# Scale and offset of an activation moved from the inner block to the outputs of the second product

## The chip, the cores and the metric

The kernel runs on one core of one Trainium2 chip. The metric is the device time of one execution in microseconds; the median over several runs counts. The names of the engines in the profile: PE is TensorE's matrix product, PEld its weight load, DVE is VectorE, ACT is ScalarE, POOL is GpSimd, SP is SyncE, which here issues the transfers.

## The reference

Local attention with a few memory keys, followed by two matrix products with a squared, scaled and shifted activation between them:

```python
# q, k, v: 4 x 8 heads x 768 x 64; per chunk of 32 queries, 16 keys to the left, 8 to the right, 8 memory keys
scores = 0.125 * q_c @ k_full.T;  a = softmax(scores);  attn = a @ v_full
x = attn.transpose(0, 2, 1, 3).reshape(3072, 512)
h = x @ w_in            # 3072 x 2048
r = np.maximum(h, 0.0)
g = s * (r * r) + b     # s and b are single numbers
out = g @ w_out         # 3072 x 512
```

All in fp32. Since s and b are single numbers, `g @ w_out` equals `s * ((r * r) @ w_out) + b * colsum(w_out)`.

## The kernel before, in words

The 3072 tokens are worked on in 8 chunks of 384. For each chunk, 16 steps run over the 16 blocks `f` of 128 columns of `w_in` (128 steps `u` in all; the list `STEPS` gives their order: 8 steps of chunk 0, then the 16 of chunk 1, then the other 8 of chunk 0, then chunks 2 to 7). A step has two parts:

- `hidden(u)`: PE multiplies the chunk's x with block f of the first matrix (L510). Each fp32 number is held as a high and a low part in a reduced fp32 form, so a product is three: four times 3 products of 384 columns. The result lies in one bank of PSUM. ACT then works on it in place: relu (L517), square (L518), affine (L519, times s plus b) and copies the high part to SBUF (`high`, L520). DVE subtracts and gets the low part `gL` (`low`, L521).
- `result(u)`: PE multiplies the high and low parts of g with block f of the second matrix (L532): three tiles of 128 tokens, three products of 512 columns each, accumulated over the 16 steps of a chunk in three banks. At the chunk's last step DVE copies each bank to SBUF (`out`, L548) and SP sends it to the output. For chunk 0, whose steps are split, ACT stores the first half (L543) and DVE adds the second (L550).

The matrices come in as 64-bit numbers. For each of their 32 tiles of 128 x 1024 words, `weight` loads the words (L485), and ACT and DVE turn them into fp32 and split them into high and low parts: ACT L487 and L496, DVE L488, L490, L492, L497. The first ten use `early` buffers, the other 22 a ring of four, `words`. All tiles stay in SBUF afterwards.

The attention of a chunk is done in four pairs of heads: scores on PE (L383), maxima on DVE (L440), exponentials on ACT (L444), a small add (L447) and the normalisation (L450) on POOL, a reciprocal (L449) and transposes (L470) on DVE, values on PE (L415).

The order of instructions on each engine is laid out beforehand by `Plan.lay`, a list scheduler: each operation has an engine, an assumed duration (`HOLD`, in ns), a priority (smaller goes first; mostly the step number or a due time) and the parts that it reads and writes. Operations marked `lock` on DVE and POOL are not put at the same time in the plan:

```python
held = o.lock and e in lock and lock[other] > t
```

The chip then runs each engine's list in that order; what an instruction waits for there are its data alone. Buffers of a ring are handed out in the order in which they were asked for.

Of the kernel before, what the change touches and what calls it, by code (L numbers as in the profile page):

```python
# [11 lines left out]
F32 = mybir.dt.float32  # L12
# [3 lines left out]
AF = mybir.ActivationFunctionType  # L16
ALU = mybir.AluOpType
# [4 lines left out]
B, H, S, D = 4, 8, 768, 64  # L22
NMEM = 8
CHUNK, LEFT, RIGHT = 32, 16, 8
DM, DFF = 512, 2048
P = 128
# [5 lines left out]
NF = DFF // P  # L32
# [14 lines left out]
APART = 3.0  # L47
LEAD = 3.5
BANKS = 8
ORDER = sorted((f + half, half, f) for f in range(NF) for half in range(2))  # L50
LATE_W = [x[1:] for x in ORDER[-NEARLY:]]

# [6 lines left out]
HOLD = dict(hidden=535, result=712, scores=306, turn=84, value=254, warm=215, group=2060, group1=1230,  # L59
            relu=388, square=388, affine=570, high=388, xhigh=388, wscale=571, whigh=536, copy=270, exp=386, keep=388, store=480, bias=500,  # L60
            low=475, affine_v=475, rec=120, max=212, flip=316, xlow=470, wlow=345, wjoin=610, wsign=612, out=600,
            small=240, norm=1010, wrest=1290, issue=440)
LATE = dict(PE=230, ACT=180, DVE=180, POOL=150, SP=0)
RATE, LAND = 400.0, 2000.0
SLOW, NSLOW = 290.0, 6
# [49 lines left out]
class Plan:  # L115
# [5 lines left out]
    def op(self, eng, kind, prio, fn, reads=(), writes=(), lock=False, size=0):  # L121
        o = Op()
        o.eng, o.hold, o.fn, o.prio, o.lock, o.n, o.size = eng, HOLD[kind], fn, prio, lock, len(self.ops), size
        o.deps, o.outs, o.vals = set(), [], []
        for part in reads:
            o.deps.update(part[1])
        for part in writes:
            o.deps.update(part[1])
            o.deps.update(part[2])
        for part in reads:  # L130
            part[2].append(o)
        for part in writes:
            part[1][:] = [o]
            part[2].clear()
        o.vals = list({id(p[0]): p[0] for p in (*reads, *writes)}.values())
        for v in o.vals:
            v.left += 1
        self.ops.append(o)
        return o
# [106 lines left out]
def body(ctx: ExitStack, tc: tile.TileContext, qkv, w1, w2, out):  # L246
    nc = tc.nc
    plan = Plan()
    op = plan.op
# [4 lines left out]
    def ring(name, n, shape, dtype):  # L254
        return Ring([const.tile(shape, dtype, name=f"{name}{i}") for i in range(n)])

    def fixed():
        return Val(Ring(None))
# [5 lines left out]
    def weight_tile(half, f):  # L264
        if (half, f) not in wts:
            i = LATE_W.index((half, f)) if (half, f) in LATE_W else -1
            wts[half, f] = const.tile([P, 2, DM], F32R, name=f"w{half}_{f}", tag=f"slot{i}" if i >= 0 else f"w{half}_{f}")
        return wts[half, f]
# [13 lines left out]
    stats = Ring([tuple(const.tile([QB, GB], F32, name=f"{n}{i}") for n in ("nmax", "den", "rden")) for i in range(4)])  # L282
    gs = Ring([(const.tile([P, TOK], F32R, name=f"gH{i}"), const.tile([P, TOK], F32R, name=f"gL{i}")) for i in range(3)])
    outs = ring("partial", 3, [P, DM], F32)

    spare = [BANKS - 1]

# [18 lines left out]
        nc.tensor.matmul(idle, ones[:, :P], ones, start=True, stop=True)  # L306


    c_id, c_aT, c_mask, c_s, c_b = (fixed() for _ in range(5))
    op("ACT", "copy", -100, lambda: nc.scalar.activation(s_sb, ones[:, :1], AF.Exp), (), (c_s[0],))  # L310
    op("POOL", "copy", -100, lambda: make_identity(nc, ident), (), (c_id[0],))
    def constants():
# [164 lines left out]
    def weight(i, half, f, due):  # L477
        src = (w1, w2)[half][f]
        raw = Early(i, 0, 2 * DM) if i < NEARLY - 6 else Val(words)
        v, w = Val(wvs), c_w[half, f]  # L480
        both = lambda: raw.tile.bitcast(I32).rearrange("p (n two) -> p n two", two=2)
        lo, hi = (lambda: both()[:, :, 0]), (lambda: both()[:, :, 1])
        bits = lambda: v.tile.bitcast(I32)
        dst = lambda a: weight_tile(half, f)[:, a, :]
        op("SP", "issue", due - 4, lambda: nc.sync.dma_start(both(), src), (), (raw["lo"], raw["hi"]), size=P * DM * 8)  # L485

        op("ACT", "wscale", due, lambda: nc.scalar.activation(v.tile, hi().bitcast(F32), AF.Copy, scale=2.0 ** -112), (raw["hi"],), (v[0],))  # L487
        op("DVE", "wlow", due, lambda: nc.vector.tensor_scalar(lo(), lo(), 29, None, ALU.logical_shift_right),  # L488
           (), (raw["lo"],), lock=True)
        op("DVE", "wjoin", due, lambda: nc.vector.scalar_tensor_tensor(bits(), bits(), 3, lo(), ALU.logical_shift_left, ALU.bitwise_or),  # L490
           (raw["lo"],), (v[0],), lock=True)
        op("DVE", "wsign", due, lambda: nc.vector.scalar_tensor_tensor(bits(), hi(), -2147483648, bits(), ALU.bitwise_and, ALU.bitwise_or),  # L492
           (raw["hi"],), (v[0],), lock=True)
        rest = half or f >= N0
        old = list(c_early[LATE_W.index((half, f))].parts.values()) if (half, f) in LATE_W else []
        op("ACT", "whigh", due, lambda: nc.scalar.activation(dst(0), v.tile, AF.Copy), (v[0],), [w["H"], *old])  # L496
        op("DVE", "wjoin", due, lambda: nc.vector.tensor_tensor(  # L497
            dst(1), v.tile, dst(0).bitcast(F32), ALU.subtract), (v[0], w["H"]), (w["L"],), lock=True)


    g_vals, h_vals, a_vals, partial = {}, {}, {}, {}

    def hidden(u):
        ch, f = STEPS[u]
        h = Val(ps, "h")
        x, w = x_vals[ch], c_w[0, f]

        def products(c):
            for n, (wi, xi) in enumerate(((0, NC_T + c), (1, c), (0, c))):
                nc.tensor.matmul(h.tile[:, :TOK], weight_tile(0, f)[:, wi, c * P:(c + 1) * P], x.tile[xi], start=(c == 0 and n == 0),  # L510
                                 stop=(c == NC_T - 1 and n == 2))

        for c in range(NC_T):
            op("PE", "hidden", u, lambda c=c: products(c), (x["H", c], x["L", c], w["H"], w["L"]), (h[0],))
        g = g_vals[u] = Val(gs)
        hp = lambda: h.tile[:, :TOK]
        op("ACT", "relu", u, lambda: nc.scalar.activation(hp(), hp(), AF.Relu), (), (h[0],))  # L517
        op("ACT", "square", u, lambda: nc.scalar.activation(hp(), hp(), AF.Square), (), (h[0],))  # L518
        op("ACT", "affine", u, lambda: nc.scalar.activation(hp(), hp(), AF.Identity, scale=s_sb, bias=b_sb), (c_s[0], c_b[0]), (h[0],))  # L519
        op("ACT", "high", u, lambda: nc.scalar.activation(g.tile[0], hp(), AF.Copy), (h[0],), (g["H"],))  # L520
        op("DVE", "low", u, lambda: nc.vector.tensor_tensor(g.tile[1], hp(), g.tile[0].bitcast(F32), ALU.subtract),  # L521
           (h[0], g["H"]), (g["L"],))

    def result(u):
        ch, f = STEPS[u]
        g, w = g_vals[u], c_w[1, f]
        first = u == 0 or STEPS[u - 1][0] != ch
        last = u + 1 == len(STEPS) or STEPS[u + 1][0] != ch

        def products(acc, t):  # L530
            for n, (gi, wi) in enumerate(((1, 0), (0, 1), (0, 0))):
                nc.tensor.matmul(acc.tile, g.tile[gi][:, t * P:(t + 1) * P], weight_tile(1, f)[:, wi, :], start=(first and n == 0), stop=(last and n == 2))  # L532

        for t in range(NT):
            if first:
                a_vals[t] = Val(ps, "acc")
            acc = a_vals[t]
            op("PE", "result", u + LAG - 0.1, lambda acc=acc, t=t: products(acc, t), (g["H"], g["L"], w["H"], w["L"]), (acc[0],))
            if not last:
                continue  # L540
            if f < NF - 1:
                o = partial[t] = Val(outs)
                op("ACT", "store", u, lambda acc=acc, o=o: nc.scalar.activation(o.tile, acc.tile, AF.Copy), (acc[0],), (o[0],))  # L543
                continue
            o = partial[t] if not ch else Val(wvs if ch == 1 else outs)
            ot = lambda o=o: o.tile
            if ch:
                op("DVE", "out", u, lambda acc=acc, ot=ot: nc.vector.tensor_copy(ot(), acc.tile), (acc[0],), (o[0],))  # L548
            else:
                op("DVE", "out", u, lambda acc=acc, ot=ot: nc.vector.tensor_tensor(ot(), acc.tile, ot(), ALU.add), (acc[0],), (o[0],))  # L550
            row = ch * TOK + t * P
            op("SP", "issue", u, lambda ot=ot, row=row: nc.sync.dma_start(out[row:row + P, :], ot()), (o[0],), (), size=P * DM * 4)

# [3 lines left out]
    made, pairs = {0}, set()  # L557
    for i, (due, half, f) in enumerate(ORDER):
        weight(i, half, f, due - 1.5)
    for u, (ch, f) in enumerate(STEPS):  # L560
        if ch not in made:
            made.add(ch)
            for c in range(H // 2):
                if (ch, c) not in pairs:
                    attend(ch, c)
            if open_ and ch + 1 < NCHUNK:
                pairs.add((ch + 1, 0))
                attend(ch + 1, 0)
            elif open_:
                open_.pop()[4]()  # L570
        hidden(u)
        result(u)
# [41 lines left out]
```

## Time and profile before

| | us |
|---|---|
| median of 3 runs | 642.14 (641.97 to 642.25) |
| span of the profiled execution | 639.8 |
| PE busy | 625.7 |
| ACT busy | 422.4 |
| DVE busy | 354.8 |
| POOL busy | 86.9 |

The page gives the span of the profiled execution, from its first to its last instruction, and no other time for it; the median of the runs lies 2.3 us above the span. In the page's second part each digit is the busy share, in tenths, of one of 40 equal slices of the span. In rows of groups the columns are line, engine, operation, output and input, shapes, count, then total busy time, mean ns of one, and the idle time before them with what ended it. In rows of the timeline and of the chain of waits the first number is the start in us, the second the duration.

### The profile page before, as it was taken

The numbers are of one execution on the slowest core, as the hardware profiler recorded it, in microseconds if no ns is written. First come the engines' busy times: TensorE is split into PE (matmuls) and PEld (weight loads), VectorE is DVE, ScalarE is ACT, GpSimd is POOL, SyncE is SP. The second block draws the span as 40 slices with busy tenths as digits, with TensorE's granted clock in tenths as the row PEclk, the third lists the DMA queues.
The fourth block names the chain that finished last, engine by engine and source line by source line (L and its number), as shares of the span: only waits on it lengthen the run. The fifth ranks groups of instructions, "written<-read, shape, count | busy, mean of one in ns | idle before, by whom it ended". The sixth has DMA issues, their size and how long they took to land.

```text
span 639.8 us, 10842 instructions
## 1 busy us (share of the span) xinstructions
PE 625.7 (98%) x3822; PEld 544.2 (85%) x3826; DVE 354.8 (55%) x1283; ACT 422.4 (66%) x1137; POOL 86.9 (14%) x140
## 2 busy tenths in 40 slices
PE   9998988999999999999999999999999999999997
PEld 5686877888888898888888988889888888989995
DVE  5999999726667355563447554473555725421112
ACT  6999898756766566666566666664666665645543
POOL 4522100101211011110011111110111100100000
PEclk9999999999999999999999999999999999999999
DMA  8933664012112011121103011120111200010001
GB/s 336 404 112 114 212 207 152 2 46 83 58 46 96 5 41 47 47 95 47 45 2 105 37 46 46 46 96 1 45 47 47 96 17 1 1 50 1 1 0 50
DMA packets 17334, 46.83 MB, mean 73 GB/s; under 512 B 1920, under 2 KB 1920, under 8 KB 17280
## 3 DMA queue, kind: packets, MB, share of 16 engines
q1 hardware_dynamic: 17280, 46.15, 20.8%
q8 instruction: 30, 0.49, 0.3%
q14 instruction: 24, 0.20, 0.1%
HBM read 39.85 MB, written 6.29 MB: 72 GB/s over the span
## 4 chain that ended last, share of the span: by engine, by line
PE 80%; DVE 10%; ACT 6%; DMA 4%; issue 1%; SPq 0%; POOL 0%; DVEq 0%
PE ps L532 37%; PE ps L510 36%; PE ps L383 4%; PE ps L415 3%; DVE wv L490 2%; DVE w L497 2%; DVE wv L492 2%; DMA early<-w 2%; ACT t L444 1%; DMA v<-qkv 1%; DVE gL L521 1%; DVE words L488 1%; ACT wv L487 1%; DMA early<-qkv 1%; ACT ps L519 1%; ACT w L496 1%
## 5 line engine op out<-in xcount | busy, mean ns | idle before, releaser
L510 PE MATMUL ps<-xH,w 128*128 128x384 f32 x1024 | 261.8, 337 | 1.3 <-DVE w L497 1.3
L532 PE MATMUL ps<-w,gH 128*128 128x512 f32 x768 | 240.0, 393 | 0.6 <-DVE w L497 0.5
L510 PEld LDWEIGHTS ps<-xH,w 128*128 128x128 f32 x1024 | 186.0, 188 | 7.6 <-DVE w L497 2.4
L521 DVE TENSOR_TENSOR gL<-ps,gH 128x384 fp32r<-128x384 f32 x128 | 70.6, 552 | 208.8 <-ACT gH L520 207.6
L517 ACT ACTIVATE ps<-ps 128x384 f32<-128x384 f32 x128 | 60.9, 475 | 173.1 <-PE ps L510 173.1
L510 PE MATMUL ps<-xL,w 128*128 128x384 f32 x512 | 174.4, 341 | 0.0
L532 PEld LDWEIGHTS ps<-w,gH 128*128 128x128 f32 x768 | 144.0, 188 | 29.4 <-DVE w L497 1.3
L532 PE MATMUL ps<-w,gL 128*128 128x512 f32 x384 | 154.9, 403 | 6.6 <-DVE gL L521 6.6
L470 DVE STREAM_TRANSPOSE aT<-t 32x128 f32<-32x128 f32 x384 | 116.2, 303 | 51.1 <-POOL t L450 46.4
L444 ACT ACTIVATE t<-t,nmax 96x128 f32<-96x128 f32 x256 | 99.3, 390 | 17.2 <-DVE nmax L440 16.9
L510 PEld LDWEIGHTS ps<-xL,w 128*128 128x128 f32 x512 | 96.1, 188 | 6.6 <-ACT w L496 0.4
L532 PEld LDWEIGHTS ps<-w,gL 128*128 128x128 f32 x384 | 72.0, 188 | 24.5 <-DVE gL L521 9.6
L519 ACT ACTIVATE ps<-ps,b_sb,s_sb 128x384 f32<-128x384 f32 x128 | 82.6, 645 | 4.2
L450 POOL TENSOR_TENSOR t<-t,rden 96x512 f32<-96x512 f32 x64 | 68.5, 1070 | 85.8 <-DVE rden L449 85.8
L447 POOL TENSOR_SCALAR rden<-den 96x4 f32<-96x4 f32 x64 | 16.0, 251 | 375.5 <-ACT t L444 372.8
L520 ACT ACTIVATE gH<-ps 128x384 fp32r<-128x384 f32 x128 | 62.9, 491 | 3.9
L518 ACT ACTIVATE ps<-ps 128x384 f32<-128x384 f32 x128 | 60.8, 475 | 4.0
L440 DVE CUSTOM_DVE_ANT_0 t<-ps,mask 96x128 f32<-96x128 f32 x256 | 56.8, 281 | 4.2 <-PE ps L383 3.8
L444 ACT ACTIVATION_READ_ACCUMULATOR t<-t,nmax 96x1 f32 x256 | 48.1, 188 | 0.0
L383 PE MATMUL ps<-raw 64*96 64x128 f32 x448 | 31.8, 279 | 0.0
L383 PEld LDWEIGHTS ps<-raw 64*96 64x96 f32 x448 | 25.3, 159 | 4.1 <-issue 0.8
L415 PEld LDWEIGHTS ps<-aT,v 128*64 128x64 f32 x448 | 19.6, 136 | 7.9 <-issue 6.6
(45 smaller groups left out, 289.3 us busy)
## 6 DMA issues: line engine op xcount, KB each, us to landing
raw<-qkv SPq DMA_DIRECT2D x28, 448.0 KB, 3.3
words<-w SPq DMA_DIRECT2D x22, 512.0 KB, 3.9
v<-qkv SPq DMA_DIRECT2D x28, 256.0 KB, 3.6
out<-partial SPq DMA_DIRECT2D x21, 256.0 KB, 2.1
early<-w SPq DMA_DIRECT2D x10, 512.0 KB, 9.9
early<-qkv SPq DMA_DIRECT2D x3, 448.0 KB, 5.8
early<-qkv SPq DMA_DIRECT2D x4, 256.0 KB, 6.4
out<-wv SPq DMA_DIRECT2D x3, 256.0 KB, 3.8
```

Of the source, the lines that this page charges most:

```text
L383: nc.tensor.matmul(scv(n)[:, j, :], raw.tile[rows, j * QB:(j + 1) * QB], raw.tile[rows, TOK + j * P:TOK + (j + 1) * P], start=True, stop=True)
L440: op("DVE", "max", a + 0.1, lambda j=j: nc.vector.tensor_tensor_reduce(t.tile[:, j, :], scv()[:, j, :], mask[:, kind(j)], -SCALE, 3.0e38, ...
L444: op("ACT", "exp", a + 0.2, lambda j=j: nc.scalar.activation(t.tile[:, j, :], t.tile[:, j, :], AF.Exp, bias=nmax()[:, j:j + 1], scale=-1.0 ...
L450: op("POOL", "norm", a + 0.25, lambda: nc.gpsimd.tensor_tensor(t.tile, t.tile, rden().unsqueeze(2).to_broadcast([QB, GB, P]), ALU.mult), [ ...
L470: nc.vector.transpose(aT.tile[gg, :, cs], t.tile[cs, :, gg])
L510: nc.tensor.matmul(h.tile[:, :TOK], weight_tile(0, f)[:, wi, c * P:(c + 1) * P], x.tile[xi], start=(c == 0 and n == 0), stop=(c == NC_T - ...
L517: op("ACT", "relu", u, lambda: nc.scalar.activation(hp(), hp(), AF.Relu), (), (h[0],))
L518: op("ACT", "square", u, lambda: nc.scalar.activation(hp(), hp(), AF.Square), (), (h[0],))
L519: op("ACT", "affine", u, lambda: nc.scalar.activation(hp(), hp(), AF.Identity, scale=s_sb, bias=b_sb), (c_s[0], c_b[0]), (h[0],))
L520: op("ACT", "high", u, lambda: nc.scalar.activation(g.tile[0], hp(), AF.Copy), (h[0],), (g["H"],))
L521: op("DVE", "low", u, lambda: nc.vector.tensor_tensor(g.tile[1], hp(), g.tile[0].bitcast(F32), ALU.subtract), (h[0], g["H"]), (g["L"],))
L532: nc.tensor.matmul(acc.tile, g.tile[gi][:, t * P:(t + 1) * P], weight_tile(1, f)[:, wi, :], start=(first and n == 0), stop=(last and n == 2))
```

## The change

`affine` on ACT goes. Its factor s is applied where the accumulators are read, at the outputs (DVE) and at chunk 0's stores (ACT). Its offset b becomes a row that is added to every output, `bc`: b times the column sums of the second matrix. POOL adds up the 16 converted tiles of the second matrix (15 adds of 128 x 1024, into a buffer of the `words` ring), two fp32 products with a matrix of ones sum over the 128 rows on PE, and ACT multiplies by b. These carry the priority 24. For chunk 0 the offset is added on POOL before the transfer.

```diff
+DUE_SUM = 24.0
...
-            small=240, norm=1010, wrest=1290, issue=440)
+            small=240, sum=2150, columns=1706, norm=1010, wrest=1290, issue=440)
...
+    bc = const.tile([P, DM], F32, name="bc")
+    ones_f = nc.const_aps.tensor(1.0, [P, P], F32)
...
+    def sums():
+
+        total, all_ = Val(words), Val(ps, "v")
+        flat = lambda f: weight_tile(1, f).bitcast(F32).rearrange("p a n -> p (a n)")
+        part = lambda f: (c_w[1, f]["H"], c_w[1, f]["L"])
+        op("POOL", "sum", DUE_SUM, lambda: nc.gpsimd.tensor_tensor(total.tile, flat(0), flat(1), ALU.add), part(0) + part(1), (total[0],), lock=True)
+        for f in range(2, NF):
+            op("POOL", "sum", DUE_SUM, lambda f=f: nc.gpsimd.tensor_tensor(total.tile, total.tile, flat(f), ALU.add), part(f), (total[0],), lock=True)
+
+        def products():
+            for a in range(2):
+                nc.tensor.matmul(all_.tile, ones_f, total.tile[:, a * DM:(a + 1) * DM], start=a == 0, stop=a == 1)
+
+        op("PE", "columns", DUE_SUM, products, (total[0],), (all_[0],))
+        op("ACT", "store", DUE_SUM, lambda: nc.scalar.activation(bc, all_.tile, AF.Identity, scale=b_sb), (all_[0], c_b[0]), (c_bc[0],))
...
-        op("ACT", "affine", u, lambda: nc.scalar.activation(hp(), hp(), AF.Identity, scale=s_sb, bias=b_sb), (c_s[0], c_b[0]), (h[0],))
...
-                op("ACT", "store", u, lambda acc=acc, o=o: nc.scalar.activation(o.tile, acc.tile, AF.Copy), (acc[0],), (o[0],))
+                op("ACT", "store", u, lambda acc=acc, o=o: nc.scalar.activation(o.tile, acc.tile, AF.Identity, scale=s_sb),
+                   (acc[0], c_s[0]), (o[0],))
...
-                op("DVE", "out", u, lambda acc=acc, ot=ot: nc.vector.tensor_copy(ot(), acc.tile), (acc[0],), (o[0],))
+                op("DVE", "out", u, lambda acc=acc, ot=ot: nc.vector.scalar_tensor_tensor(ot(), acc.tile, s_sb, bc, ALU.mult, ALU.add),
+                   (acc[0], c_s[0], c_bc[0]), (o[0],))
...
-                op("DVE", "out", u, lambda acc=acc, ot=ot: nc.vector.tensor_tensor(ot(), acc.tile, ot(), ALU.add), (acc[0],), (o[0],))
+                op("DVE", "out", u, lambda acc=acc, ot=ot: nc.vector.scalar_tensor_tensor(ot(), acc.tile, s_sb, ot(), ALU.mult, ALU.add),
+                   (acc[0], c_s[0]), (o[0],))
+                op("POOL", "norm", u + 1, lambda ot=ot: nc.gpsimd.tensor_tensor(ot(), ot(), bc, ALU.add), (c_bc[0],), (o[0],), lock=True)
...
     for i, (due, half, f) in enumerate(ORDER):
         weight(i, half, f, due - 1.5)
+    sums()
```

More of the change, by code (lines that the diff above doesn't have):

```diff
@@ L306, in warm @@
         nc.tensor.matmul(idle, ones[:, :P], ones, start=True, stop=True)
-    c_id, c_aT, c_mask, c_s, c_b = (fixed() for _ in range(5))
+    c_id, c_aT, c_mask, c_s, c_b, c_bc = (fixed() for _ in range(6))
     op("ACT", "copy", -100, lambda: nc.scalar.activation(s_sb, ones[:, :1], AF.Exp), (), (c_s[0],))
```

## The prediction

> **What bounds the kernel now.** I read the page's first two parts, then the chain of waits, piece by piece for the first 120 us.
>
> ```profile
> span 639.8 us, 10842 instructions
> PE 625.7 (98%) x3822; PEld 544.2 (85%) x3826; DVE 354.8 (55%) x1283; ACT 422.4 (66%) x1137; POOL 86.9 (14%) x140
> ...
> PE   9998988999999999999999999999999999999997
> ...
> DVE  5999999726667355563447554473555725421112
> ACT  6999898756766566666566666664666665645543
> ...
> PEclk9999999999999999999999999999999999999999
> ...
> PE 80%; DVE 10%; ACT 6%; DMA 4%; issue 1%; SPq 0%; POOL 0%; DVEq 0%
> ```
>
> The span is 639.8 us; the median of the runs is 642.14 us, so 2.3 us lie around it, and I add every change to 642.14. TensorE (PE) looks full throughout, with an undisturbed clock, but the chain gives it 80%, not 98%: in the first seven slices (16 us each) ScalarE (ACT) and VectorE (DVE) are full too. The pieces of the chain show who hands over to whom:
>
> ```profile
> 31.32 0.64 ACT ps L519
> ...
> 35.63 0.65 ACT ps L519
> ...
> 41.28 0.65 ACT ps L519
> ...
> 49.77 0.55 ACT ps L519
> ...
> 53.86 0.65 ACT ps L519
> ...
> 55.09 0.69 DVE w L497
> ...
> 112.45 0.48 DVE gL L521
> ...
> 112.97 2.33 PE ps L532 x9
> ...
> 117.41 2.09 PE ps L532 x9
> ...
> 140.21 2.29 PE ps L532 x9
> ```
>
> So there are three stages: ACT sets the pace to 55 us, DVE (the conversion of the weights) to 113 us, and PE from there to the end. L519 is the affine step that goes. It is worth something only where ACT is on this chain, and in the tail.
>
> **The affine step, removed.** Over the whole kernel it is 82.6 us of ACT:
>
> ```profile
> L519 ACT ACTIVATE ps<-ps,b_sb,s_sb 128x384 f32<-128x384 f32 x128 | 82.6, 645 | 4.2
> DVE w L497 <- ACT w L496: 1.7, 3, 1.2
> DVE gL L521 <- ACT gH L520: 0.9, 2, 0.7
> ```
>
> The last two rows are DVE's waits in the window 8 to 115 us. In the PE stage the step is hidden by PE, and its removal gives nothing. In the first 55 us five of them, 0.64 + 0.65 + 0.65 + 0.55 + 0.65 = 3.1 us, lie on the chain. But DVE is next: its work up to 113 us stays as it is, so a faster ACT can shorten this stretch only by the time that DVE waits for ACT, 1.7 + 0.9 = 2.6 us. Ends 0 (the planner spends it on another order) and 2.6; I take 2.3, since 3.1 us removed exceeds the sum of the waits, and leave 0.3 for gaps of the new order.
>
> In the tail the last hidden block goes through relu, square, affine, high and low before PE may go on:
>
> ```profile
> 631.97 0.65 ACT L519 ACTIVATE ps<-ps,b_sb,s_sb 128x384 f32<-128x384 f32 x1
> 632.39 0.63 PE L532 MATMUL ps<-w,gH 128*128 128x512 f32 x2
> 633.78 0.50 PE L532 MATMUL ps<-w,gL 128*128 128x512 f32 x1 [0.76 <-DVE gL L521]
> ```
>
> PE waits 0.76 us there, longer than the 0.65 removed: gain 0.65.
>
> **The two fp32 products with the ones, added on PE.** They fall in the stage where PE is full, so their whole time counts. No 128x128 fp32 product of 512 columns is in the trace; the nearest row is the fp32 score product:
>
> ```profile
> 139.10 1.12 PE L383 MATMUL ps<-raw 64*96 64x128 f32 x16
> ```
>
> Sixteen of 64 rows, issued in pairs for the two halves of the array: eight pairs, 0.14 us per 128 columns. Two products of 512 columns over all rows are then 8 x 0.14 = 1.1 us. That is the lower end. Upper end: the entry columns=1706 in the diff, plus the 0.2 us by which the nine result products take longer behind an fp32 group (2.29 against 2.09): 1.9. I take 1.7, as this product is twice as high and fills the array alone. The Trainium skill, "FP8 and Floating Point Precision", section TensorE Precision Notes, says that true fp32 makes four passes; with the 2.09 us for nine results an estimate is 2 x 4 x 0.23 = 1.9 us. By that the sum would be 0.2 us higher; no row here shows a full-height fp32 product.
>
> **The sums on GpSimd, added.** Fifteen adds of 128x1024. Their duration comes from the normalisation and the small add:
>
> ```profile
> L450 POOL TENSOR_TENSOR t<-t,rden 96x512 f32<-96x512 f32 x64 | 68.5, 1070 | 85.8 <-DVE rden L449 85.8
> L447 POOL TENSOR_SCALAR rden<-den 96x4 f32<-96x4 f32 x64 | 16.0, 251 | 375.5 <-ACT t L444 372.8
> 105.83 0.69 DVE L492 SCALAR_TENSOR_TENSOR wv<-words,wv 128x512 int32<-128x512 int32 x1
> 117.69 0.22 POOL L447 TENSOR_SCALAR rden<-den 96x4 f32<-96x4 f32 x1 [49.60 <-ACT t L444]
> 156.15 0.68 DVE L548 COPY wv<-ps 128x512 f32<-128x512 f32 x1
> ```
>
> Twice 1070 ns is 2.1 us; by the slope between the two rows, (1070 - 251) / 508 = 1.6 ns an element, 0.25 + 1.65 = 1.9. Fifteen are 28 to 32 us. The total needs a words buffer, and it is the last in line: it gets the one of the nineteenth of 22 loads, whose last reader is the L492 at 105.83. So the adds can start at about 106.5, on a GpSimd (POOL) that sits idle for 49.6 us until 117.69. With the two pairs of small add and normalisation that come in between (2 x 2 x 1.3 us) they end at about 140 to 145; products and store make it 148. The first reader of bc is the output of step 23, at 156.15: some 8 us to spare. Behind that output on DVE wait the next maxima and gL, and for its bank of PSUM the next accumulation. I cost this wait at nothing, under the cover of these 8 us.
>
> What the adds do to DVE while weights are still being converted is the open cost. The planner keeps certain POOL and DVE instructions apart (lock), but only in its own plan; on the chip the adds are held by data alone. What an overlap costs:
>
> ```profile
> 36.73 1.04 POOL L450 TENSOR_TENSOR t<-t,rden 96x512 f32<-96x512 f32 x1 [1.15 <-DVE rden L449]
> 37.35 0.97 DVE L497 TENSOR_TENSOR w<-wv,w 128x512 fp32r<-128x512 f32 x1
> 39.45 0.69 DVE L490 SCALAR_TENSOR_TENSOR wv<-wv,early 128x512 int32<-128x512 int32 x1
> 39.52 1.52 POOL L450 TENSOR_TENSOR t<-t,rden 96x512 f32<-96x512 f32 x1 [0.29 <-DVE rden L449]
> 161.00 2.52 DVE L470 STREAM_TRANSPOSE aT<-t 32x128 f32<-32x128 f32 x8 [1.16 <-POOL t L450]
> 161.06 0.22 POOL L447 TENSOR_SCALAR rden<-den 96x4 f32<-96x4 f32 x1
> ```
>
> Where POOL was first, L497 took 0.97 instead of 0.69 us and ended 0.55 us behind POOL's end at 37.77; where DVE was first, POOL took 1.52 instead of 1.04. So the two wait for each other whole. The transposes do not take part (0.22 beside them, as alone), so the adds after the weights cost DVE nothing. Between 106.5 and 116 us DVE has a dozen instructions that do. But the late weights serve steps 20 and up and have time; what PE needs is gL, which does not wait for POOL unless it stands behind one that does:
>
> ```profile
> 107.04 0.55 DVE L521 TENSOR_TENSOR gL<-ps,gH 128x384 fp32r<-128x384 f32 x1
> ...
> 115.22 0.55 DVE L521 TENSOR_TENSOR gL<-ps,gH 128x384 fp32r<-128x384 f32 x1
> ```
>
> Its product runs at 117.41, so this last gL has 1.6 us of slack. The first add (2.1 us) falls at the gL of 107.04, and DVE has maxima ready that do not contend. Ends: 0 (one add there, filled) and 3 x 2.1 - 1.6 = 4.7 (three more adds ahead of the small add at 117.69). Nearest is the pair of rows above, where DVE lost 0.3 of POOL's 1.04 us; 0.3 of three adds is 1.9, less part of the slack: I take 1.0.
>
> **The small edits.**
>
> ```profile
> L550 DVE TENSOR_TENSOR partial<-ps,partial 128x512 f32<-128x512 f32 x3 | 1.9, 685 | 0.0
> L548 DVE COPY partial<-ps 128x512 f32<-128x512 f32 x18 | 11.7, 686 | 3.3 <-PE ps L532 3.2
> ```
>
> Outputs: DVE now reads a second tensor and a scalar, and 685 against 686 says that this costs nothing, in the tail too. The three stores of chunk 0 with a scale may cost ACT something, but they fall in the stage in which DVE sets the pace: nothing. The add of bc to chunk 0 on POOL (three of about 1.1 us) delays only output transfers in SP's queue, whose next loads are far ahead of need: nothing. One PSUM bank for the column sums for some 2 us can move an attention group by a step: nothing, PE has other work.
>
> **The sum.** -2.3 - 0.65 + 1.7 + 1.0 = -0.25: 641.9 us.
>
> **Rivals.** (1) Faster: DVE's waits go whole and the adds find DVE busy with what does not contend: -2.6 - 0.65 + 1.4 + 0 = -1.9, 640.3. For it: the maxima that wait for a free DVE and the weights' spare time. Best corner, with 1.1 on PE: 640.0. (2) Slower, by the lock: if the plan puts two or more further adds ahead of POOL's first small add, the chip runs them back to back from 106.5, and DVE's weight instructions, with gL behind them, stand still: -1.25 + 4.7 gives 645.6 with three, -1.25 + 2.6 gives 643.5 with two; with one or none it is covered. The rule behind it is in the Trainium skill, "SBUF — State Buffer", section Who interferes with whom: whichever issues first keeps the shared port pair for its whole instruction and the other fully blocks. The rows at 37 and 39 us agree. (3) Slower, by the new wait: if the adds take 2.5 us (15 x 0.5 = 7.5 us more) and DVE holds POOL up by 3.5 us more, bc is 3 us late, the output of step 23 waits for it and PE for the output's bank: 644.9. (4) It does not do what it says: the planner's new order loses the 2.3 us at the start, and DVE paces as before: 644.2.
>
> **Numbers.** About 0.2%, 1.3 us, is what a measurement here can tell from no change. Forecast (640.9 to 643.4) 0.36; rival 1 0.32; rival 2 0.20; rival 3 0.05; rival 4 0.07. Faster 0.32, same 0.36, slower 0.32. The forecast's own range is 640.9 to 643.4. For 8 in 10 the range goes from just below the best corner, 639.6, to just past rival 2 with three adds, 646.0.
>
> **What would show it.** The chain passes from ACT to DVE earlier than 55 us and from DVE to PE near 111 us; DVE's waits for ACT before that are near zero; PE waits less than 0.2 us at the end; two products of some 1.7 us together stand near 146 us with PE full around them. Weight instructions of DVE of 1.5 to 2.8 us beside long adds would show rival 2; a DVE output waiting for ACT's bc, rival 3. I am wrong if the adds start much earlier or later than 106 us, or take other than about 2 us, or if the new order leaves PE gaps after 120 us.

## The result, and the profile after

The changed kernel takes 714.51 us (median; 714.34 to 714.96) against 642.19 us: ratio 1.113, 95% interval 1.112 to 1.115. It is 72 us slower; forecast were 641.9 us and a range that ended at 646.0. The direction was that of some of the rivals, the size that of none.

The page of the changed kernel, first two parts and the chain:

```profile
span 712.2 us, 10776 instructions
PE 630.7 (89%) x3829; PEld 547.5 (77%) x3833; DVE 381.9 (54%) x1283; ACT 346.2 (49%) x1010; POOL 128.5 (18%) x158
...
PE   9987100279999999999999999999999999999997
...
DVE  5999999353116767344735473556555564422112
ACT  6977630083335645554444453455445554433332
POOL 4510049730001213011101120111111111100000
PEclk9999655599999999999999999999999999999999
...
PE 79%; DVE 9%; POOL 6%; ACT 3%; DMA 2%; issue 1%; SPq 0%; DVEq 0%; POOLq 0%; ACTq 0%
```

ACT is relieved as intended (346.2 us busy instead of 422.4), and PE has 5 us more to do. But in slices 5 to 8 (18 us each) PE does next to nothing, and POOL, with 6% on the chain, is new there. The waits name it, and PE's and POOL's timelines show it (start, duration, instruction; in brackets the idle time before):

```profile
PE ps L515 <- POOL words L511: 64.5, 1, 64.5
```

```profile
72.98 0.63 PE L551 MATMUL ps<-w,gH 128*128 128x512 f32 x2
138.08 3.78 PE L515 MATMUL ps<-words,const-float32-1.0 128*128 128x512 f32 x4 [64.48 <-POOL words L511]
141.66 1.49 PE L462 MATMUL ps<-ident,t 96*128 96x96 f32 x8
```

```profile
98.37 2.40 POOL L509 TENSOR_TENSOR words<-w,w 128x1024 f32<-128x1024 f32 x1 [58.52 <-ACT wv L490]
100.84 37.19 POOL L511 TENSOR_TENSOR words<-words,w 128x1024 f32<-128x1024 f32 x14
```

One wait of 64.5 us: after the eight steps of chunk 0 PE stands at the column products until POOL has added all 16 tiles. The third row of PE says why nothing else is done meanwhile: chunk 1's transposes (L462) come right behind the column products. In the kernel before, all eight groups of them (L459) ran between 27 and 69 us; here none runs between 26 and 141 us.

The cause is in `sums()` and in the way in which `Ring` hands out buffers. Banks of PSUM of one kind are given in the order in which they were asked for (`self.next.get(v.kind, 0) == v.n`). The column sums ask for a bank of kind "v" with `Val(ps, "v")`, and `sums()` is called ahead of the loop in which chunk 1 asks. The transposes and values of the attention use kind "v" too. So in the plan no transpose of chunk 1 can have a bank before the column products have had theirs, and these wait for the last weight and 15 adds. The chip then keeps the plan's order. The second half of chunk 0 cannot fill the gap either: its hidden blocks ask for banks of kind "h" behind those of chunk 1.

DVE's rows at that place show the second effect, which the prediction had as a rival:

```profile
97.55 0.69 DVE L495 SCALAR_TENSOR_TENSOR wv<-words,wv 128x512 int32<-128x512 int32 x1
98.15 0.42 DVE L491 TENSOR_SCALAR words<-words 128x512 int32<-128x512 int32 x1
98.60 2.71 DVE L493 SCALAR_TENSOR_TENSOR wv<-wv,words 128x512 int32<-128x512 int32 x1
101.24 2.82 DVE L500 TENSOR_TENSOR w<-wv,w 128x512 fp32r<-128x512 f32 x1
103.98 2.83 DVE L495 SCALAR_TENSOR_TENSOR wv<-words,wv 128x512 int32<-128x512 int32 x1
106.74 2.56 DVE L491 TENSOR_SCALAR words<-words 128x512 int32<-128x512 int32 x1
```

From the first add on, the same DVE instructions take 2.6 to 2.8 instead of 0.4 to 0.7 us: each waits for most of an add, and the adds, with 37.19 / 14 = 2.66 us instead of 2.40, wait for DVE in turn. So on the chip an instruction waits not for its data alone, as the section on the kernel before has it: DVE and POOL also wait for each other. The Trainium skill, "SBUF — State Buffer", section Who interferes with whom, has this as a lock that the first holds for its whole instruction while the other fully blocks; 2.82 - 0.69 = 2.1 us, most of an add, agrees.

### The profile page after: what moved, and what is told of

It is laid out like the page before. It is cut to its first block, busy times and chain, and to the rows that moved or that the text cites. A ratio compares the mean times of both kernels' runs of the same rounds, so it can differ in the third digit from the quotient of the medians.

```text
span 712.2 us, 10776 instructions
## 1 busy us (share of the span) xinstructions
PE 630.7 (89%) x3829; PEld 547.5 (77%) x3833; DVE 381.9 (54%) x1283; ACT 346.2 (49%) x1010; POOL 128.5 (18%) x158
## 4 chain that ended last, share of the span: by engine, by line
PE 79%; DVE 9%; POOL 6%; ACT 3%; DMA 2%; issue 1%; SPq 0%; DVEq 0%; POOLq 0%; ACTq 0%
PE ps L551 36%; PE ps L530 35%; POOL words L511 5%; PE ps L386 4%; PE ps L418 3%; DVE wv L493 3%; DVE w L500 2%; DVE wv L495 2%; DMA early<-w 1%; ACT t L447 1%; DVE words L491 1%; DMA early<-qkv 1%; DVE gL L540 1%; PE ps L515 1%; DVE t L443 1%
## 5 line engine op out<-in xcount | busy, mean ns | idle before, releaser
L515 PE MATMUL ps<-words,const-float32-1.0 128*128 128x512 f32 x4 | 3.8, 1100 | 64.5 <-POOL words L511 64.5
L511 POOL TENSOR_TENSOR words<-words,w 128x1024 f32<-128x1024 f32 x14 | 36.2, 2583 | 1.1
L499 ACT ACTIVATE w<-wv 128x512 fp32r<-128x512 f32 x32 | 20.1, 629 | 25.2 <-DVE wv L495 24.7
```

Source lines behind the costliest of these rows:

```text
L511: op("POOL", "sum", DUE_SUM, lambda f=f: nc.gpsimd.tensor_tensor(total.tile, total.tile, flat(f), ALU.add), part(f), (total[0],), lock=True)
```

## The experiments

**The line of banks.** `own_bank` gives the column sums a kind of their own, which also takes them out of the limit on how many banks the attention may hold:

```diff
+        if kind == "c":
+            return True
         return n("h", 0) < 2
...
-        total, all_ = Val(words), Val(ps, "v")
+        total, all_ = Val(words), Val(ps, "c")
```

> The changed kernel, but the bank of PSUM for the column sums is asked for in a line of its own instead of the line in which the transposes and values of the attention ask. Theory A (the line: the column sums were asked for ahead of chunk 1's attention, banks of a line are handed out in the order asked, so chunk 1's transposes and values cannot be planned before the column sums): PE no longer stops for 64 us, the time comes back to 642 to 648 us. Rival B (the 15 adds and the DVE instructions that wait for them hold PE up by themselves): the adds still take some 40 us and the time stays above 690 us.

Measured: 648.95 us (ratio to the kernel before 1.011, 1.010 to 1.013). That is as theory A said: 65.6 of the 72 us go with the line. A loss of 7 us stays. `asked_later`, below, keeps the kind and the limit and moves the place alone.

`no_adds` keeps the line, and leaves out 14 of the 15 adds:

```diff
-            ... flat(0), flat(1), ALU.add), part(0) + part(1), (total[0],), lock=True)
-        for f in range(2, NF):
-            op("POOL", "sum", ...)
+            ... flat(NF - 1), flat(NF - 2), ALU.add), part(NF - 1) + part(NF - 2), (total[0],), lock=True)
```

> The changed kernel with the line of banks as it is, but 14 of the 15 adds left out: the total is the sum of the last two tiles alone (the column sums are wrong by the rest). Theory A: PE still stops before the column sums, now until the last weight tiles are converted and one add is done, near 110 us instead of 138: about 685 us. Rival B: without the adds PE is not held up, 640 to 646 us.

Measured: 687.94 us (one run), near the 685 of theory A. PE's timeline in this kernel:

```profile
108.14 3.78 PE L513 MATMUL ps<-words,const-float32-1.0 128*128 128x512 f32 x4 [35.31 <-POOL words L509]
111.72 1.49 PE L462 MATMUL ps<-ident,t 96*128 96x96 f32 x8
```

PE still stops, for 35.3 us, and the transposes still stand behind. So of the wait of 64.5 us some 35 are for the last weights and one add, and 29 for the adds that follow and slow the last weights down.

`asked_later` is the changed kernel with `sums()` called once chunk 1's attention has asked for its banks:

```diff
-    sums()
     for u, (ch, f) in enumerate(STEPS):
...
+        if u == starts[1]:
+            sums()
         hidden(u)
```

> The changed kernel with the column sums asked for at another place: after chunk 1's attention instead of before it, in the same line of banks as it was. Theory A (the place in the line decides who has to wait): chunk 1 is free, now the attention of chunk 2 stands behind the column sums; it is needed later, so the loss is a fraction of the 65 us: 650 to 660 us. Rival B (what counts is only that the column sums use a bank of that line at all): above 690 us.

Measured: 659.95 us (one run), at the edge of what A said. No wait for the column products is left, but the time is 11 us more than in `own_bank`: now chunk 2's attention is late, and PE waits for gL behind it three times between 167 and 198 us:

```profile
169.18 0.50 PE L551 MATMUL ps<-w,gL 128*128 128x512 f32 x1 [2.03 <-DVE gL L540]
183.48 0.80 PE L551 MATMUL ps<-w,gL 128*128 128x512 f32 x1 [2.04 <-DVE gL L540]
197.80 0.50 PE L551 MATMUL ps<-w,gL 128*128 128x512 f32 x1 [2.13 <-DVE gL L540]
```

With the same kind and the same limit, the place in the line alone is worth 714.51 - 659.95 = 54.6 us.

**The affine step.** `no_affine` is the kernel before without it:

```diff
-        op("ACT", "affine", u, lambda: nc.scalar.activation(hp(), hp(), AF.Identity, scale=s_sb, bias=b_sb), (c_s[0], c_b[0]), (h[0],))
```

> The kernel before with the affine step left out and nothing in its place (s and b are missing from the result). What its removal alone is worth. The prediction's terms say -2.3 us at the start and -0.65 us in the tail: 639.2 us. Rival: the planner's new order does not use the time at the start, only the tail gains: 641.5 us.

Measured: 639.82 us (ratio 0.997, 0.996 to 0.998): -2.0 us where the terms said -2.95. DVE's waits for ACT in the window 8 to 115 us, and PE at 83 us and, in the last two rows, in the tail:

```profile
DVE gL L520 <- ACT gH L519: 0.5, 2, 0.3
...
DVE w L497 <- ACT w L496: 0.4, 1, 0.4
```

```profile
83.01 0.50 PE L531 MATMUL ps<-w,gL 128*128 128x512 f32 x1 [2.14 <-DVE gL L520]
83.34 0.83 PE L531 MATMUL ps<-w,gH 128*128 128x512 f32 x2
83.97 0.63 PE L531 MATMUL ps<-w,gL 128*128 128x512 f32 x1
84.40 1.05 PE L531 MATMUL ps<-w,gH 128*128 128x512 f32 x2
...
631.25 0.63 PE L531 MATMUL ps<-w,gH 128*128 128x512 f32 x2
631.96 0.50 PE L531 MATMUL ps<-w,gL 128*128 128x512 f32 x1
```

DVE's waits for ACT fell from 2.6 to 0.9 us, and PE's gap in the tail from 0.76 to 0.08 us. The two are worth 2.4 us. Against that stands a gap of 2.1 us at 81 us that the kernel before did not have, where the new order puts a gL late, and behind it products that take 0.63 instead of 0.40 us: the granted clock is 0.57 in the 4 us after it. What this gap costs in the end is not shown. PE's waits for gL over the whole kernel fell all the same, as these rows of the kernel before and of `no_affine` show (us in total, times, longest):

```profile
PE ps L532 <- DVE gL L521: 6.6, 9, 0.9
PE ps L531 <- DVE gL L520: 4.3, 5, 2.1
```

**What the products and the small edits cost.** `own_no_adds` is `own_bank` without 14 of the adds, the one that is left being of the last two tiles.

> late_adds with 14 of the 15 adds left out (the column sums hold the last two tiles only); the two products, the store and the new outputs stay. Against no_affine (639.8 us) it shows what the products and the other small edits cost: theory A 1.9 us for the two products, 641 to 642 us. If it is as late_adds, the adds after the weights cost nothing; if it is at 640 or below, the products are hidden after all.

Measured: 642.04 us (ratio 1.000, 0.999 to 1.001): 2.2 us over `no_affine`. The products of `own_bank`, at full clock, are 1.88 us:

```profile
157.63 1.88 PE L517 MATMUL ps<-words,const-float32-1.0 128*128 128x512 f32 x4
```

They are not hidden. The 0.3 us that is left for the other edits is no more than the runs of one kernel differ by. With the bank and the adds out of the way the change is worth nothing: -2.0 + 2.2.

**The adds.** So the adds cost `own_bank` 648.95 - 642.04 = 6.9 us. Its rows on DVE, POOL and PE:

```profile
109.65 0.68 DVE L502 TENSOR_TENSOR w<-wv,w 128x512 fp32r<-128x512 f32 x1
110.25 2.63 DVE L493 TENSOR_SCALAR words<-words 128x512 int32<-128x512 int32 x1
...
114.25 2.62 DVE L493 TENSOR_SCALAR words<-words 128x512 int32<-128x512 int32 x1
```

```profile
109.67 2.92 POOL L513 TENSOR_TENSOR words<-words,w 128x1024 f32<-128x1024 f32 x1
112.68 1.01 POOL L452 TENSOR_SCALAR rden<-den 96x4 f32<-96x4 f32 x2
113.76 2.82 POOL L513 TENSOR_TENSOR words<-words,w 128x1024 f32<-128x1024 f32 x1
```

```profile
121.60 0.80 PE L553 MATMUL ps<-w,gL 128*128 128x512 f32 x1 [5.42 <-DVE gL L542]
122.19 1.05 PE L553 MATMUL ps<-w,gH 128*128 128x512 f32 x2
```

```profile
121.00:126.00 5.00, 4.40 (x11) 3.54 (x12) 3.84 (x13) 0.63 (x1) 3.84 (x3) 0.50 0.00 0
```

Two DVE instructions wait 2.2 us each for an add, gL stands behind them, and PE is idle for 5.4 us (4.4 of them for these two waits, the other 1.0, by this difference, for the plan's order); then its clock is 0.50 for the next 5 us (the last row is the window of all engines, the clock is its third number from the end).

`late_adds` moves the adds so that they meet no such DVE instruction:

```diff
-            ... flat(0), flat(1), ALU.add), part(0) + part(1), ...
-        for f in range(2, NF):
+            ... flat(NF - 1), flat(NF - 2), ALU.add), part(NF - 1) + part(NF - 2), ...
+        for f in range(NF - 2):
```

> own_bank with the adds in another order: the first add takes the last two tiles of the second matrix, so no add can start before the weights are converted, and no add meets a DVE instruction that shares the port. Theory A (own_bank's excess of some 7 us over the kernel before is DVE held up by the adds at 107 to 117 us, PE idle behind it for 5.4 us and at half clock for 5 us more): the gap goes, 641 to 643 us. Rival B (the excess is the new order of the plan, or the output of step 23 waiting for bc, which now comes later): 645 us or more.

Measured: 649.4 us (ratio 1.012, 1.010 to 1.013). Not as A said, though the gap that A named is gone. Two others came:

```profile
150.28 0.50 PE L553 MATMUL ps<-w,gL 128*128 128x512 f32 x1 [1.45 <-DVE gL L542]
...
158.79 3.45 PE L517 MATMUL ps<-words,const-float32-1.0 128*128 128x512 f32 x4 [4.04 <-POOL words L513]
```

```profile
129.20 19.75 POOL L513 TENSOR_TENSOR words<-words,w 128x1024 f32<-128x1024 f32 x8
149.04 0.51 POOL L452 TENSOR_SCALAR rden<-den 96x4 f32<-96x4 f32 x2
```

```profile
149.29 0.47 DVE L454 RECIPROCAL rden<-rden 96x4 f32<-96x4 f32 x2 [7.10 <-POOL rden L452]
149.68 0.54 DVE L542 TENSOR_TENSOR gL<-ps,gH 128x384 fp32r<-128x384 f32 x1
```

An add takes 19.75 / 8 = 2.47 us, so 15 of them, with the attention's POOL work among them, last from 116.8 to 158.7 us, and PE reaches its column products 4 us too early; behind this wait they take 3.45 instead of 1.88 us. The first gap comes from the adds too: POOL's small add (L452) stands behind eight of them, DVE's reciprocal waits 7.1 us for it, and gL stands behind the reciprocal. The gaps and the longer products make 1.45 + 4.04 + 1.57 = 7.1 us, of 649.4 - 642.04 = 7.4 over `own_no_adds`. So B's half sentence on lateness was right, with the column products and not the output of step 23 as the place. Started early, the adds meet DVE; started late, they do not finish in time.

`half_adds` tests the second: the same order with adds of half the width (only the high parts) and one product. The planner's durations for them are halved too (1250 and 853 ns).

```diff
-        flat = lambda f: weight_tile(1, f).bitcast(F32).rearrange("p a n -> p (a n)")
+        flat = lambda f: weight_tile(1, f)[:, 0, :].bitcast(F32)
...
+        half = lambda: total.tile[:, :DM]
...
-            for a in range(2):
-                nc.tensor.matmul(all_.tile, ones_f, total.tile[:, a * DM:(a + 1) * DM], start=a == 0, stop=a == 1)
+            nc.tensor.matmul(all_.tile, ones_f, half(), start=True, stop=True)
```

> late_adds with adds of half the width: only the high parts of the tiles are summed, the low parts are left out of the column sums, and one product takes the place of two. The adds still start after the weights are converted. Theory A (late_adds pays 6.9 us over own_no_adds because 15 full adds of 2.45 us cannot be done between the last weight at 117 us and the place of the column sums near 155 us; with 1.2 to 1.3 us each they are done near 140): PE's gap of 4 us goes; own_no_adds (642.0) less one product (0.9) is 641.1 us. Rival B (adds beside the attention cost by their number, or delay its normalisation, whatever their length): 643 us or more.

Measured: 641.0 us (ratio 0.998, 0.997 to 0.999), as A said (its 6.9 us for `late_adds` is `own_bank`'s number; it should be 7.4). PE's gaps at 116, 149 and 155 us are gone, and the adds are short:

```profile
126.07 13.62 POOL L514 TENSOR_TENSOR words<-words,w 128x512 f32<-128x512 f32 x10
```

So the loss of `late_adds` is the length of its adds. That the loss of `own_bank` is its early adds rests on the rows above and on the gap at 116 us, which is gone when they start later.

**PE's clock in the long wait.** `warm_wait` is the changed kernel with idle products in front of the column sums:

```diff
         def products():
+            for _ in range(280):
+                nc.tensor.matmul(all_.tile, ones[:, :P], ones, start=True, stop=True)
             for a in range(2):
```

> The changed kernel with 280 idle products (bf16 ones, into the bank that the column sums use next) in PE's queue ahead of the column sums, about 61 of the 64 us that PE waits there. Nothing else is moved. Theory A: part of the 72 us is PE's clock, at 0.50 after the wait; with PE busy the column products take 1.9 instead of 3.8 us and the attention behind them runs at full clock: 710 to 712 us. Rival B: behind the wait PE is held by other engines, so a faster clock shortens nothing but the column products, or not even these: 713 to 714.5 us.

Measured: 714.99 us, with runs from 712.92 to 716.52, so unclear. The idle products ended 3.2 us too soon, and the clock was down again (0.63 from 138 to 142 us). A share of the clock in the 72 us is not shown. In the changed kernel the clock is 0.50 from 138 to 142 us and 0.87 in the next 4 us, so an estimate of the most that it can be is 4 x 0.50 + 4 x 0.13 = 2.5 us. Why the runs of `warm_wait` differ by more than those of the others was not tried; over the whole run the granted clock was 0.998 in the two shorter ones and 0.990 in the two longer.

**A version without column sums.** `fold_b` is the kernel before without the affine step; b/s is added where the high and low parts are made, and s multiplies the outputs (one DVE reciprocal and one product of 128 x 1 at the start give b/s):

```diff
-        op("ACT", "affine", ...)
-        op("ACT", "high", u, lambda: nc.scalar.activation(g.tile[0], hp(), AF.Copy), (h[0],), (g["H"],))
-        op("DVE", "low", u, lambda: nc.vector.tensor_tensor(g.tile[1], hp(), g.tile[0].bitcast(F32), ALU.subtract), ...)
+        op("ACT", "ghigh", u, lambda: nc.scalar.activation(g.tile[0], hp(), AF.Identity, bias=b_sb), (h[0], c_b[0]), (g["H"],))
+        op("DVE", "low", u, lambda: nc.vector.scalar_tensor_tensor(g.tile[1], hp(), b_sb, g.tile[0].bitcast(F32), ALU.add, ALU.subtract), ...)
...
-                op("DVE", "out", u, lambda acc=acc, ot=ot: nc.vector.tensor_copy(ot(), acc.tile), ...)
+                op("DVE", "out", u, lambda acc=acc, ot=ot: nc.vector.tensor_scalar(ot(), acc.tile, s_sb, None, ALU.mult), ...)
```

> The kernel before without the affine step; instead b/s is added where the high part is copied (a bias on ACT) and where the low part is formed (a scalar in the DVE instruction), and s multiplies the outputs. No column sums, no adds, no extra product. If the affine step is worth what the prediction said and the bias costs ACT little: 639.5 us. If the bias makes the high copy longer by as much as a quarter of the affine step or the planner's order is worse: 641 to 642 us.

Measured: 639.38 us (ratio 0.996, 0.995 to 0.997), faster than the kernel before and the changed one. Groups of this kernel:

```profile
L523 DVE SCALAR_TENSOR_TENSOR gL<-ps,b_sb,gH 128x384 fp32r<-128x384 f32 x128 | 78.3, 612 | 200.2 <-ACT gH L522 174.4 <-PE ps L534 25.0
...
L522 ACT ACTIVATE gH<-ps,b_sb 128x384 fp32r<-128x384 f32 x128 | 74.4, 581 | 4.1
```

The two that take the scalar in are 0.06 to 0.09 us longer (552 and 491 ns before), and the affine step's 645 ns is gone. Its 639.38 us are no more than the 639.82 of `no_affine`, which leaves s and b out.

## Why the prediction was wrong

- **The bank (the step that failed).** The prediction put a term at nothing: "One PSUM bank for the column sums for some 2 us can move an attention group by a step: nothing." I costed the bank by how long it is held. What it cost was its place: 65.6 us (`own_bank`). For the buffer of `words` I had used the same rule, that the total is the last in line; for the banks I did not ask who stands behind. It was to be read from the code alone, and no row of the profile before shows it.
- **The affine step.** -2.3 and -0.65 were said, -2.0 in all was measured (`no_affine`). The waits of DVE for ACT went as described, though not whole (1.7 of 2.6 us), and the tail gained its 0.7. The 0.4 us between these 2.4 and the 2.0 may be the new order's gap at 81 us and the clock behind it, for which the prediction had left 0.3 us; that is not shown.
- **The products.** 1.7 said, 1.88 in the trace, and 2.2 in the time together with the small edits. The four passes of the Trainium skill, "FP8 and Floating Point Precision", section TensorE Precision Notes, gave 1.9, nearer than the row that I took as the lower end.
- **The adds and the lock.** 1.0 said, 6.9 measured. The mechanism was rival 2's, with 2.2 us for each DVE instruction that meets an add; in `own_bank` two did, and PE was idle for 5.4 us. But rival 2 asked for two further adds ahead of POOL's first small add and called one covered; in `own_bank` one stands there (109.67, the small add at 112.68) and one behind. The 0.3 of an add was misread: L497 at 37.35 came 0.42 us before POOL's end, so its row shows the rest of one instruction and not a share; the two in `own_bank` came 0.5 to 0.6 us into an add. Too small was the cover: gL had 1.6 us of slack in the kernel before, and none in the new order. The clock behind an idle PE, some 2 us (0.50 for 5 us with PE 4.4 us busy), was not in the sum at all.
- **The adds' length.** 1.9 to 2.1 us were said, 2.47 measured. An end at 140 to 145 us became 156 (`own_bank`) and 159 (`late_adds`); in `own_bank` 5.6 us of that is POOL waiting for DVE's reciprocal before 122 us. So the cover of 8 us under which the new wait cost nothing was not there. In `own_bank` PE still did not wait, for the plan had its column products at 157.63; `late_adds`, whose adds start 10 us later, shows that wait. That "the adds after the weights cost DVE nothing" did not hold there either: the transposes kept their pace (2.52 us for eight at 129 us), but the reciprocal waited for POOL's small add behind the adds, and gL with it.
- **The outputs.** 685 against 686 ns said that a second tensor costs nothing; with the scalar it is 746 (L570 of `own_bank`). In `fold_b` an output with the scalar and no second tensor takes 746 as well, so it goes with the scalar.

From the changed kernel over `own_bank`, `own_no_adds` and `no_affine` to the kernel before, the steps are bank 65.6, adds 6.9, products and the rest 2.2, affine step -2.0. Being differences between neighbours they must add up to the whole (72.7 us; 72.3 with the kernel before as it was measured beside the changed one), so their sum proves nothing by itself.

## What to carry to other kernels

Where a planner hands out buffers in the order in which they were asked for, a new user's cost is not how long it holds one but who asked after it and what it waits for itself: find that line before costing anything else. Before moving work off a busy engine, see whether it can be folded into instructions that exist on both sides (here a bias and a scalar operand) instead of into new ones on a third engine. An engine that sits idle beside a busy neighbour is not free when the two block each other.

## What the runs showed of the hardware that I had not expected

DVE and POOL take turns strictly: in the changed kernel, from 98.6 to 128 us, each of DVE's weight instructions took 2.56 to 2.83 us instead of 0.42 to 0.69 beside adds of 2.4 us, and the 14 adds behind the first took 2.66 us on average. That holds for the shift of a single tensor (L491, 2.56) as well as for those that read two.

The granted clock of PE fell after gaps of 2.0 and 2.1 us (0.57 to 0.59 in the next 4 us, `no_affine` and `asked_later`), but not after another of 2.1 us in `asked_later` nor after one of 1.6 us in the changed kernel; what decides is not shown. By an estimate from these numbers a gap of 2.1 us can so cost 2.1 + 4 x 0.43 = 3.8 us.
